# An attention-and-MLP kernel whose instruction order comes from a planner: VectorE units placed by bank, MLP output parked in SBUF, zero products in TensorE's pauses

## The chip, the cores and the metric

The kernel runs on one core of a Trainium2 chip. The metric is the device time of one execution in microseconds (us), lower is better. Three runs of the kernel before gave 899.79, 900.54 and 901.49 us; the median is 900.54 us.

## The reference, cut to what matters

```python
def _A_ref(x, wqkv, wo):                       # S = 2048 tokens, D = 512, H = 32 heads of Dh = 16
    q, k, v = split(x @ wqkv)
    p = softmax((q @ k.T) * Dh ** -0.5)        # per head, 2048 x 2048
    return merge_heads(p @ v) @ wo
def _B_ref(x, w1, b1, w2, b2):                 # F = 1792
    h = gelu(layernorm(x) @ w1 + b1)           # tanh form
    return h @ w2 + b2
xn = layernorm(x)
return x + _A_ref(xn, wqkv, wo) + _B_ref(xn, w1, b1, w2, b2)
```

So there are 32 x 2048 x 2048 exponentials, the two small products around each, and an MLP over the same tokens.

## The kernel before, in words

Work is cut into 32 groups: 4 quarters of 512 queries (`qt`), and in each 8 sets of 4 heads (`g`). For one group and one of 16 blocks of 128 keys (`k`) there are 4 score tiles of 128 x 512, one for each head. TensorE makes a score tile with one product of 32 rows (`qk`, from `kt` and `qz`); products of different heads stand in different rows of the array and run together. Most score tiles are exponentiated by ScalarE: two or three PSUM banks at a time, a *tile* of the plan (`build_tile`, banks 0 to 2 and 3 to 4 in turn, result in the 15 slots of `p_sb`). In groups 2 to 31 four of the sixteen key blocks (`KD`) go to VectorE instead: it makes the exponential from the bits of float16 numbers. One such block has 4 *units*: each reads one score tile out of PSUM and writes int16 (`f1`, result `x_sb`), and then four additions over all 4 heads (`f2`, results `tb_x` and `x_sb`) give five terms. The exponentials are multiplied with the values (`pv`, four products of 32 columns that run together, a *row* below) and gathered over a whole group in PSUM bank 6. After a group VectorE copies that bank out (`osb`), the sums of the softmax go through HBM and back to be inverted and spread over the partitions (`ldram`, `lc`, `rc`, `rdram`, `rlb`), and VectorE multiplies (`ont`).

Banks 5 and 7 (`misc`) serve everything else: the scores of the VectorE units, the projections, and the MLP. A resource `one` lets only one user other than the units hold a `misc` bank at a time. In each quarter the MLP makes 14 blocks of its hidden layer (`build_mlp`: four products each, VectorE adds the bias and writes `ht`), one gelu over all of it on ScalarE, and then `build_out` makes for each of 4 token blocks one chain of products into one bank: the input itself, 14 products of `ht` with `w2`, the bias, and 8 of the attention's heads with `wo`. VectorE copies the bank to `ot`, and it is stored. In the last quarter the chain leaves the last two heads to `build_final`, which adds them at the end.

Nothing of this order is fixed in the code. `_Plan` simulates the engines with estimated durations; at each step it takes, for each engine, the ready operation with the smallest `prio` among those that can start within `TOL` of the first, with a bonus `KEEP` for TensorE operations of the same kind as the last (scores, values, or dense). Which tile a unit rides on was fixed ahead (`rider`): its score product was issued with a tile's, and the tile then needed a free `misc` bank to start. Where `_Plan` finds TensorE idle, `fill` may put products with zeros there; before, only ahead of 15 us of the plan. On the chip each engine runs its instructions in the planned order, held by semaphores.

Of the kernel before, what the change touches and what calls it, by code (L numbers as in the profile page):

```python
# [22 lines left out]
P = 128  # L23
DH = 16
HS = 4
# [26 lines left out]
class _Op:  # L52

    __slots__ = ("eng", "dur", "fn", "ndeps", "outs", "prio", "acq", "rel", "lat", "ready", "end",
                 "done", "dense", "mode", "seq")
# [5 lines left out]
class _Plan:  # L61
# [9 lines left out]
    TOL = 0.2  # L71
    KEEP = 2.0
# [16 lines left out]
    def add(self, eng, dur, fn, deps=(), prio=0.0, acq=(), rel=(), lat=0.0, dense=0.0, nb=0.0,  # L89
            mode=None):  # L90
        op = _Op()
        op.eng, op.dur, op.fn, op.prio, op.lat, op.dense = eng, dur, fn, prio, lat, dense
# [12 lines left out]
        self.ops.append(op)  # L105
        return op
# [16 lines left out]
    def run(self):  # L123
# [5 lines left out]
        left = len(self.ops)  # L129
        self.mode = None  # L130
        while left:
# [20 lines left out]
            if op.eng == "PE" and self.fill is not None:  # L152
                for dur, fn in self.fill(free["PE"], t):
                    self.cur = "PE"
                    fn()
                    free["PE"] += dur
                t = max(t, free["PE"])
            ready[op.eng].remove(op)
            for res, key in op.acq:
# [5 lines left out]
            self.now = t  # L165
# [15 lines left out]
            if op.dense:  # L181
                self.dense_log.append((t, op.dense))
            lag = self.PELAT if op.eng == "PE" else self.LAT
            for o in op.outs:
# [4 lines left out]
            left -= 1  # L189
        self.free = free  # L190

    dense_log = ()
# [239 lines left out]
def kernel(  # L432
# [136 lines left out]
    OUT0, OUT1, HLO = 0.4, 0.7, 0.42  # L569
    LEAD = 7  # L570
    start = [T0]
    for g in range(NG):
        start.append(start[-1] + (31.0 if not KD_OF[g] else 24.0) + (1.1 if g % NS != 7 else 1.5))
# [365 lines left out]
    rider = {}  # L939
# [3 lines left out]
    todo = []  # L943
    for g in range(NG):
        t = tiles_of[g]
        nd = len(KD_OF[g])
        for y, k in enumerate(KD_OF[g]):
            todo.append((g, k, {0, 1, 2, 3}, t[0] + len(t) * y / nd - LEAD))
    for i, (b0, n, u0) in enumerate(tiles):
        if not todo or todo[0][3] > i:  # L950
            continue
        g, k, js, _ = todo[0]
        fits = js - {units[u][2] for u in range(u0, u0 + n)}
        if fits:
            j = min(fits, key=lambda j: (j - units[u0][2] - n) % HS)
            rider[i] = (g, k, j)
            js.discard(j)
            if not js:
                todo.pop(0)
    assert not todo  # L960

    def build_tile(i):
# [3 lines left out]
        gd, kd, jd = rider.get(i, (None, None, None))  # L966
        key = ("d", i)

        def fqk():
            for x, (g, k, j) in enumerate(us):  # L970
                qk(b0 + x, g, k, j)
            if kd is not None:
                qk(misc.bank(key), gd, kd, jd)
# [4 lines left out]
        acq = [(res[b0 + x], ("t", i)) for x in range(n)]  # L978
        if kd is not None:
            need_q(gd)  # L980
            deps.update(qk_deps(gd, kd))
            deps.add(va_op[NT - 1])
            acq.append((misc, key))
        q = add("PE", pen(1), fqk, list(deps) + [qk_prev[0]], dl - 43.0, acq=acq, mode="q")
# [3 lines left out]
        if kd is not None:  # L988
            qk_last.setdefault(gd, []).append(q)
            dve_unit(gd, kd, jd, q, dl, key)  # L990
# [17 lines left out]
    def build_pv(u0):  # L1008
        g, k, _ = units[u0]

        def fpv():
            pv(g, k, [(va[:, k, :], lambda j: p_sb[:, unit_slot[u0 + j], :])])
        o = add("PE", pen(1), fpv, set([unit_exp[u0 + j] for j in range(HS)]
                                       + [va_op[k], va_op[min(k + 1, NT - 1)]]),
                due(u0 + 4) - 37.0, acq=((o_ready, g),), mode="p")
        for j in range(HS):
            pv_of_unit[u0 + j] = o
        pv_ops[g].append(o)
# [4 lines left out]
    ib_of, p1_ops = {}, {}  # L1023

    def dve_unit(g, k, j, q, dl, key):
        if (g, k) not in ib_of:
            ib_of[g, k] = ib_n[0]
            ib_n[0] += 1
        n_ = ib_of[g, k]
        sl = n_ % NI  # L1030

        def f1():
            I(nc.vector.tensor_scalar(out=ib[sl][:, j, :], in0=ps[:, misc.bank(key), :],  # L1033
                                      scalar1=LEVEL, scalar2=0.0, op0=ALU.add, op1=ALU.max))
        ins = p1_ops.setdefault((g, k), [])
        ins.append(add("DVE", dve(QW), f1, [q] + list(ib_use.get(n_ - NI, ()))
                       + list(xn_op.values()), dl - 800.0, rel=(misc.giver(key),)))
        if len(ins) == HS:
            dve_terms(g, k, n_, ins, dl)

    def dve_terms(g, k, n_, ins, dl):
# [7 lines left out]
        for t in range(1, TERMS):  # L1049
# [8 lines left out]
            a = add("DVE", dve(HS * QW, 0.26), f2, ins + list(tb_use.get(x - NTB, ())), dl + t - 20.0)  # L1058
# [3 lines left out]
            if len(rows) == 2 or t == TERMS - 1:  # L1062
                o = add("PE", pen(len(rows)), lambda rows=rows: pv(g, k, rows),
                        deps + [va_op[NT - 1], vs_op[k]], dl + 5.0 - 37.0, acq=((o_ready, g),),
# [88 lines left out]
    def build_mlp(qt):  # L1153
        lo, hi = (qts(qt, 0.30), qts(qt, 0.78)) if qt == 0 else (qts(qt, HLO), qts(qt, 0.78))
# [46 lines left out]
        def fg():  # L1201
            for h0 in (0, half):
# [6 lines left out]
    def build_out(qt, gl):  # L1209
        del h_use[:]  # L1210
        last = qt == NQT - 1
        for c in range(TQ):
# [5 lines left out]
            if last:  # L1218
                pr = ts_(NG - 1, -0.8 + 0.35 * c)
                gs = gs[:-2]  # L1220
            xr = dma("SP", x_r[:, qi % 2, :], x2[qi * P:(qi + 1) * P, :],
                     list(x_use.get(qi - 2, ())), pr - 10, nb=pr - 20)
            steps = [(ident_bf[:], x_r[:, qi % 2, :])]
            steps += [(ht[:, fc, cs], w2_sb[:, fc, :]) for fc in range(FC)]
            steps += [(ones_bf[0:1, 0:P], b2_sb[0:1, :])]
            steps += [(ont[:, g % NON, cs], wo_pad[:, (g % NS) // 2, g % 2, :]) for g in gs]
            m = gl
            for f0 in range(0, len(steps), 3):
                part = steps[f0:f0 + 3]

                def fn(part=part, f0=f0, key=key, n=len(steps)):
                    for y, (a, b) in enumerate(part):
                        I(nc.tensor.matmul(ps[:, misc.bank(key), :], lhsT=a, rhs=b,  # L1233
                                           start=(f0 + y == 0), stop=(f0 + y == n - 1)))
                deps = [m]
                if f0 == 0:
                    deps += [xr, ld_w2, ld_b2] + [on_op[g] for g in gs] + ld_wo
                m = add("PE", mmd(len(part)), fn, deps, pr,
                        acq=((one, key), (misc, key)) if f0 == 0 else (), dense=float(len(part)))
                if f0 == 0:  # L1240
                    x_use[qi] = (m,)
                if f0 <= FC < f0 + 3 and c == TQ - 1:
                    h_use.append(m)
            for g in gs:
                ont_use.setdefault(g, []).append(m)
            if not last:
                e = add("DVE", dve(D), lambda qi=qi, key=key: I(nc.vector.tensor_copy(
                    ot[:, qi % 2, :], ps[:, misc.bank(key), :])), [m, ot_use.get(qi - 2)], pr - 500,
                    rel=(one, misc.giver(key)))
                ot_use[qi] = dma("SP", o2[qi * P:(qi + 1) * P, :], ot[:, qi % 2, :], (e,), pr)  # L1250
            else:
                acc_op[c] = add("DVE", dve(D), lambda c=c, key=key: I(nc.vector.tensor_copy(
                    acc[:, c, :], ps[:, misc.bank(key), :])), [m], pr - 500,
                    rel=(one, misc.giver(key)))
# [24 lines left out]
    gl = {0: build_mlp(0)}  # L1279
    ti = pend = 0  # L1280
    for g in range(NG):
        qt, s = divmod(g, NS)
        stop = end_unit[g]
# [9 lines left out]
        if s == (NS - 1 if qt < NQT - 1 else NS - 3):  # L1293
            build_out(qt, gl[qt])
            if qt + 1 < NQT:
                gl[qt + 1] = build_mlp(qt + 1)
# [3 lines left out]
    log = I.dense_log = []  # L1300

    def fill(t0, t1):
        got = []
        t = max(t0, 2.5)
        while t0 < T0 and t + 0.25 < t1:
            def fn():
                I(nc.tensor.matmul(ps[:, OB, :], lhsT=zeros_bf[:], rhs=ones_bf[:],
                                   start=True, stop=True))
            got.append((0.216, fn))
# [46 lines left out]
```

## Time and profile before

| | |
|---|---|
| median of 3 runs | 900.54 us |
| profiled execution, its own time | 901.28 us |
| its span, first to last instruction | 899.4 us |
| busy: TensorE, VectorE, ScalarE | 774.4, 773.4, 773.0 us (each 86% of the span) |
| granted TensorE clock, mean | 0.938 of full |

The rows below come from one profiled execution. A row of the timeline has the start, the length, the engine, the line of the kernel, what is written and read, and in brackets how long the engine had been idle and what ended that. PE is TensorE, DVE is VectorE, ACT is ScalarE, SP issues the DMAs. Rows that follow each other on an engine are merged and counted (x4). TensorE's busy time is modelled, and products overlap in it, so what a product costs is read from the distance of starts.

### The profile page before, as it was taken

What the parts mean: (1) busy time and instruction counts of PE and PEld (TensorE: products, weight loads), DVE (VectorE), ACT (ScalarE), POOL (GpSimd) and SP (SyncE); (2) the same over time, 40 slices, a digit from 0 to 9 for tenths busy, and PEclk for the clock granted to TensorE, in tenths of its full rate; (3) what the DMA queues carried; (4) which work ended last, traced back from release to release, by engine and by line L of the source; (5) the groups of instructions that cost most, each with busy time, mean ns of one, the idle gap of its engine ahead of it and who ended that gap; (6) DMA issues with size and microseconds to landing.
All of it is one profiled execution on the core that took longest, in us unless ns stands there. A gap on an engine that the chain in (4) does not pass through costs nothing.

```text
span 899.4 us, 17244 instructions
## 1 busy us (share of the span) xinstructions
PE 774.4 (86%) x6866; PEld 244.3 (27%) x6948; DVE 773.4 (86%) x1330; ACT 773.0 (86%) x667; POOL 53.1 (6%) x153
## 2 busy tenths in 40 slices
PE   8998889968889998986879987996878898899796
PEld 3332222212222232221222222321222222222222
DVE  8657999979998899996988899997888789999583
ACT  4896889999998889889998789889998789998792
POOL 2200000000000000000000000000000000000000
PEclk9997899989899999997899999998799999899898
DMA  5300121000000100110000010210000010021000
GB/s 164 100 1 19 28 57 26 15 13 20 20 20 26 43 26 18 42 28 19 19 20 26 20 36 15 48 38 19 3 20 30 26 38 19 9 60 32 19 20 28
DMA packets 54810, 27.65 MB, mean 31 GB/s; under 512 B 40645, under 2 KB 50630, under 8 KB 54722
## 3 DMA queue, kind: packets, MB, share of 16 engines
q1 hardware_dynamic: 52562, 24.76, 10.1%
q10 hardware_dynamic: 2160, 1.70, 0.6%
q8 instruction: 56, 0.92, 0.4%
q14 instruction: 32, 0.26, 0.1%
HBM read 23.85 MB, written 2.61 MB: 29 GB/s over the span
## 4 chain that ended last, share of the span: by engine, by line
DVE 36%; PE 32%; ACT 16%; issue 9%; DMA 6%; SPq 0%; POOL 0%; ACTq 0%; DVEq 0%
ACT p_sb L999 14%; DVE x_sb L1033 14%; PE ps L933 11%; PE ps L915 10%; DVE tb_x L1054 7%; PE ps L1233 7%; DMA rlb<-rdram 4%; DVE x_sb L1054 4%; DVE ht L1195 3%; ACT ht L1204 1%; PE ps L812 1%; DMA rdram<-rc 1%; DVE ont L1101 1%; DVE osb L1087 1%; PE ps L740 1%
## 5 line engine op out<-in xcount | busy, mean ns | idle before, releaser
L999 ACT ACTIVATE p_sb<-ps 128x1024 bf16<-128x1024 f32 (+1 forms) x640 | 732.6, 1234 | 99.4 <-PE ps L915 93.4
L1033 DVE TENSOR_SCALAR x_sb<-ps 128x512 int16<-128x512 f32 x480 | 323.9, 683 | 55.7 <-PE ps L915 54.9
L915 PE MATMUL ps<-qz,kt 32*128 32x512 bf16 x2048 | 282.2, 405 | 82.8 <-ACT p_sb L999 70.2
L1054 DVE TENSOR_SCALAR tb_x<-x_sb 128x2048 int16<-128x2048 int16 x320 | 215.6, 684 | 6.2 <-PE ps L933 4.4
L933 PE MATMUL ps<-p_sb,va 128*32 128x512 bf16 x1568 | 163.8, 410 | 0.2
L915 PEld LDWEIGHTS <-kt 32*128 32x128 bf16 x2048 | 75.6, 91 | 300.4 <-issue 295.6
L933 PE MATMUL ps<-tb_x,vs 128*32 128x512 f16 x1280 | 127.5, 410 | 7.1 <-DVE tb_x L1054 6.4
L1054 DVE TENSOR_SCALAR x_sb<-x_sb 128x2048 int16<-128x2048 int16 x160 | 109.3, 683 | 2.0 <-PE ps L933 1.3
L933 PEld LDWEIGHTS <-va 128*32 128x32 bf16 x2048 | 50.2, 95 | 128.1 <-issue 124.6
L933 PEld LDWEIGHTS <-vs 128*32 128x32 bf16 x1920 | 59.2, 98 | 83.6 <-issue 64.7
L933 PE MATMUL ps<-x_sb,vs 128*32 128x512 f16 x640 | 67.9, 412 | 3.1 <-DVE x_sb L1054 3.0
L1188 PE MATMUL ps<-yT,w_r 128*128 128x512 bf16 x194 | 56.4, 383 | 8.8 <-DVE x_sb L1033 5.7
L1108 POOL TENSOR_SCALAR okt<-lc 128x16 f32<-128x16 f32 x31 | 12.5, 404 | 785.9 <-DMA lc<-ldram 785.9
L1233 PE MATMUL ps<-w_sb,ht 128*128 128x512 bf16 x198 | 56.2, 391 | 2.7 <-issue 2.1
L933 PE MATMUL ps<-x_sb,va 128*32 128x512 f16 x480 | 51.4, 414 | 2.6 <-DVE osb L1087 2.5
L1195 DVE TENSOR_SCALAR ht<-ps,b_sb 128x512 bf16<-128x512 f32 x56 | 41.7, 744 | 1.0 <-PE ps L1188 0.8
L1101 DVE TENSOR_TENSOR ont<-osb,rlb 128x512 bf16<-128x512 f32 x31 | 21.3, 686 | 15.0 <-DMA rlb<-rdram 15.0
L1233 PE MATMUL ps<-wo_pad,ont 128*128 128x512 bf16 x113 | 31.3, 382 | 1.0 <-issue 1.0
L1188 PEld LDWEIGHTS <-w_r 128*128 128x128 bf16 x224 | 19.6, 97 | 38.9 <-issue 25.3
L1233 PEld LDWEIGHTS <-ht 128*128 128x128 bf16 x224 | 17.9, 98 | 32.0 <-issue 19.7
L1204 ACT ACTIVATE ht<-ht 128x3584 bf16<-128x3584 bf16 x8 | 25.1, 3183 | 0.0
L1087 DVE COPY osb<-ps 128x512 f32<-128x512 f32 x31 | 21.2, 684 | 4.5 <-PE ps L933 4.4
(88 smaller groups left out, 304.8 us busy)
## 6 DMA issues: line engine op xcount, KB each, us to landing
rlb<-rdram SPq DMA_DIRECT2D x31, 256.0 KB
w_r<-in_B_w_dram SPq DMA_DIRECT2D x56, 128.0 KB
x_r<-in_A_x_dram SPq DMA_DIRECT2D x16, 128.0 KB
w_sb<-in_B_w_dram SPq DMA_DIRECT2D x1, 1792.0 KB
out_dram<-ot SPq DMA_DIRECT2D x12, 128.0 KB
x_sb<-in_A_x_dram SPq DMA_DIRECT2D x2, 512.0 KB
wkv<-in_A_wqkv_dram ACTq DMA_DIRECT2D x1, 512.0 KB
x_sb<-in_A_x_dram ACTq DMA_DIRECT2D x1, 512.0 KB
```

Source lines behind the costliest of these rows:

```text
L915: I(nc.tensor.matmul(ps[:, bank, :], lhsT=kt[lo:lo + 32, s // 2, k * P:(k + 1) * P], rhs=qz[lo:lo + 32, (qt * NB + s // 2) % NQB, s % 2, : ...
L933: I(nc.tensor.matmul(ps[32 * j:32 * j + 32, o_bank[g], :], lhsT=vals[:, h * VS:h * VS + 32], rhs=wts(j), start=st, stop=(pv_left[g] == 0), ...
L999: I(nc.scalar.activation(p_sb[:, s0:s1, :].rearrange("p a b -> p (a b)"), ps[:, b0:b0 + n, :].rearrange("p a b -> p (a b)"), AF.Exp, scale ...
L1033: I(nc.vector.tensor_scalar(out=ib[sl][:, j, :], in0=ps[:, misc.bank(key), :], scalar1=LEVEL, scalar2=0.0, op0=ALU.add, op1=ALU.max))
L1054: I(nc.vector.tensor_scalar(out=tb[x % NTB].rearrange("p j q -> p (j q)"), in0=ib[sl].rearrange("p j q -> p (j q)"), scalar1=float(SHIFT[t ...
L1087: e0 = add("DVE", dve(QW), lambda: I(nc.vector.tensor_copy(osb[:, i2, :], ps[:, o_bank[g], :])), pvs + before, pr - 1000, rel=(o_ready if ...
L1101: e4 = add("DVE", dve(QW), lambda: I(nc.vector.tensor_tensor(out=ont[:, slot, :], in0=osb[:, i2, :], in1=rlb[:], op=ALU.mult)), [e3] + lis ...
L1108: I(nc.gpsimd.tensor_scalar(out=okt[:, 0, :], in0=lc[:, i2, :], scalar1=L_MIN, scalar2=None, op0=ALU.is_ge))
L1188: I(nc.tensor.matmul(ps[:, misc.bank(key), :], lhsT=w1_r[:, n % NW1, jc, :], rhs=yT[:, jc, :], start=(jc == 0), stop=(jc == JC - 1)))
L1195: I(nc.vector.tensor_scalar(out=ht[:, fc, :], in0=ps[:, misc.bank(key), :], scalar1=b1_sb[:, fc:fc + 1], scalar2=None, op0=ALU.add))
L1204: I(nc.scalar.activation(out=hv, in_=hv, func=AF.Gelu_apprx_tanh, scale=1.0))
L1233: I(nc.tensor.matmul(ps[:, misc.bank(key), :], lhsT=a, rhs=b, start=(f0 + y == 0), stop=(f0 + y == n - 1)))
```

## The change

- **Units.** `rider` is no longer fixed ahead. When a tile is scheduled, the function `ride` decides whether a unit goes with it: only when a `misc` bank is free at that time of the plan, unless the unit is late (`LATE`). While ScalarE is in gelu (`gelu_end`), units may go with no tile at all: operations marked `spare` that the plan may drop. `build_dve` builds a block's VectorE work ahead, without the number of the tile.
- **MLP output.** The chain of each token block is cut in two. `build_down` (input, 14 products with `w2`, bias) follows the gelu in the same quarter, and VectorE copies the bank to `acc` in SBUF (the space of `wkv`). `build_out` has the 8 head products alone, later; VectorE adds `acc` while it empties the bank. Chains are issued in parts of four products and no longer three. There are 16 more emptyings of a bank than before.
- **Zero products.** `fill` also works after the start: where the plan has TensorE idle, and either the pause is long or less than `NEED` products lie in the last 3.4 us, products with zeros are added into the open sum of bank 6.
- **Numbers of the plan.** `TOL`, `KEEP`, the times of the MLP (`HLO`, `HHI`, `DN0`, `DN1`, `OUT0`, `OUT1`) and the lead of each kind of operation change.

```diff
-    TOL = 0.2
-    KEEP = 2.0
+    TOL = 0.25
+    KEEP = 0.5
...
+    def ride(i, alone=None):
...
+        def f(_, take=False, give=None):
+            if alone is not None:
+                if take:
+                    g, k, js, _, late = todo[0]
+                    return attach(g, k, js, js, True, key, misc(key))
+                if (not todo or gelu_end[0] <= I.now or todo[0][3] - AHEAD > tile_now[0]
+                        or not all(o.done for o in qk_deps(*todo[0][:2]))):
+                    return None
+                free = misc(key)
+                return None if free is None or free >= gelu_end[0] else free
...
+            must = late - len(js) <= i
+            free = misc(key)
+            if not take:
+                return free if must else 0.0
+            if free is None or not (must or free <= I.now + 0.05):
+                return None
...
-        q = add("PE", pen(1), fqk, list(deps) + [qk_prev[0]], dl - 43.0, acq=acq, mode="q")
+        q = add("PE", pen(1), fqk, list(deps) + [qk_prev[0]], dl - QO, acq=acq, mode="q")
...
+    def build_down(qt, gl):
...
+            pr = qts(qt, DN0 + DN1 * c)
+            steps = [(ident_bf[:], x_r[:, qi % 2, :])]
+            steps += [(ht[:, fc, cs], w2_sb[:, fc, :]) for fc in range(FC)]
+            steps += [(ones_bf[0:1, 0:P], b2_sb[0:1, :])]
...
+            acc_op[c] = add("DVE", dve(D), lambda c=c, key=key: I(nc.vector.tensor_copy(
+                acc[:, c, :], ps[:, misc.bank(key), :])),
+                [m] + wait, pr - 500, rel=(one, misc.giver(key)))
...
+            steps = [(ont[:, g % NON, cs], wo_pad[:, (g % NS) // 2, g % 2, :]) for g in gs]
...
+            acc_op[c] = e = add("DVE", dve(D), lambda c=c, key=key, dst=dst: I(
+                nc.vector.tensor_tensor(out=dst, in0=ps[:, misc.bank(key), :], in1=acc[:, c, :],
+                                        op=ALU.add)),
...
-        while t0 < T0 and t + 0.25 < t1:
+        while t + 0.25 < t1:
+            if t0 > T0:
+                if o_open[0] is None:
+                    break
+                if (t1 - t0 < 2.0
+                        and sum(d for (a, d) in log[-40:] if a > t - 3.4) >= NEED):
+                    t += 0.1
+                    continue
...
```

Three places show how the order moves. Line numbers shift by some 50: `f1` is L1033 before and L1085 now, `f2` L1054 and L1108, `rc` L1094 and L1148, `ont` L1101 and L1155, the score products L915 and L921, the products of value rows L933 and L939.

VectorE around the gelu of the second quarter. Before:

```order
L1054 TENSOR_SCALAR x_sb<-x_sb 128x2048
L1054 TENSOR_SCALAR tb_x<-x_sb 128x2048 x2
L796 TENSOR_SCALAR qc<-ps 128x512
L801 TENSOR_SCALAR qz<-qc,mask 128x512 x2
L1101 TENSOR_TENSOR ont<-osb,rlb 128x512
L1033 TENSOR_SCALAR x_sb<-ps 128x512 x4
```

And now (`wkv` in the last row is the space that `acc` uses):

```order
L1108 TENSOR_SCALAR x_sb<-x_sb 128x2048
L1085 TENSOR_SCALAR x_sb<-ps 128x512 x2
L1108 TENSOR_SCALAR tb_x<-x_sb 128x2048
...
L1085 TENSOR_SCALAR x_sb<-ps 128x512 x2
L1108 TENSOR_SCALAR x_sb<-x_sb 128x2048
L1108 TENSOR_SCALAR tb_x<-x_sb 128x2048
L802 TENSOR_SCALAR qc<-ps 128x512
L1155 TENSOR_TENSOR ont<-osb,rlb 128x512
...
L1298 COPY wkv<-ps 128x512
```

Pairs of units stand in a row with the additions of their block between them, and the first emptying of an MLP chain follows shortly behind; before, no unit stood between the last additions and `ont`.

VectorE between the inverted sums `rc` and the multiplication `ont` of the 25th group before, with 7 instructions between:

```order
L1094 RECIPROCAL rc<-lc 128x16
L1033 TENSOR_SCALAR x_sb<-ps 128x512
L1054 TENSOR_SCALAR tb_x<-x_sb 128x2048 x2
L1033 TENSOR_SCALAR x_sb<-ps 128x512
L1054 TENSOR_SCALAR x_sb<-x_sb 128x2048
L1054 TENSOR_SCALAR tb_x<-x_sb 128x2048
L1033 TENSOR_SCALAR x_sb<-ps 128x512
L1101 TENSOR_TENSOR ont<-osb,rlb 128x512
```

And of the 23rd group now, with 26 instructions between:

```order
L1148 RECIPROCAL rc<-lc 128x16
L1108 TENSOR_SCALAR tb_x<-x_sb 128x2048
L1085 TENSOR_SCALAR x_sb<-ps 128x512 x2
...
L1108 TENSOR_SCALAR x_sb<-x_sb 128x2048
L1085 TENSOR_SCALAR x_sb<-ps 128x512
L1155 TENSOR_TENSOR ont<-osb,rlb 128x512
```

Over the 31 groups that go through HBM, 15 had at most 12 VectorE instructions between `rc` and `ont`; now 8 have.

VectorE at the very end, before:

```order
L1130 STREAM_TRANSPOSE ont<-on_t 128x512
L1135 TENSOR_SCALAR okl<-ta 128x16
...
L1141 TENSOR_REDUCE okr<-okl 128x1
L1252 COPY wkv<-ps 128x512
L1273 TENSOR_TENSOR yT<-ps,wkv 128x512 x4
```

And now:

```order
L1184 STREAM_TRANSPOSE ont<-on_t 128x512
L1189 TENSOR_SCALAR okl<-ta 128x16
...
L1195 TENSOR_REDUCE okr<-okl 128x1
L1344 TENSOR_TENSOR yT<-ps,wkv 128x512 x4
```

The emptying of the last MLP chain no longer stands between the last heads and the final sums.

More of the change, by code (lines that the diff above doesn't have):

```diff
@@ L128, in run @@
                 ready[op.eng].append(op)
-        left = len(self.ops)
+        left = sum(not op.spare for op in self.ops)
         self.mode = None
@@ L1220, in build_out @@
                 gs = gs[:-2]
[L1221 to L1243, printed above, removed]
@@ L1282 @@
         qt, s = divmod(g, NS)
+        for y in range(len(KD_OF[g])):
+            build_dve(g, y)
         stop = end_unit[g]
```

203 lines of the change are left out of this document (130 added, 73 removed).

## The prediction

> **What bounds the kernel now.** I began with the page's span and busy times, then asked the waits who waits for whom, then cut the span into stretches of about one group (19 or 20 tiles of ScalarE), and last read the timeline in the worst of them.
>
> ```profile
> span 899.4 us, 17244 instructions
> ...
> PE 774.4 (86%) x6866; PEld 244.3 (27%) x6948; DVE 773.4 (86%) x1330; ACT 773.0 (86%) x667; POOL 53.1 (6%) x153
> ```
>
> ```profile
> ACT p_sb L999 <- PE ps L915: 93.4, 145, 3.7
> PE ps L915 <- ACT p_sb L999: 70.2, 139, 5.2
> DVE x_sb L1033 <- PE ps L915: 54.9, 65, 5.4
> DVE ont L1101 <- DMA rlb<-rdram: 15.0, 11, 3.0
> PE ps L933 <- DVE osb L1087: 2.5, 8, 0.6
> ```
>
> The three engines are equally busy, so no total names the bound. The waits do: ScalarE idles 93.4 us for score products, TensorE 70.2 us for banks that ScalarE still reads, VectorE 54.9 us for unit scores. ScalarE's exponentials are the same 640 before and after; so the time falls only where ScalarE's idle time does, and I go by stretches (columns: length, then busy time and count of PE, weight loads, DVE, ACT and POOL, then the clock).
>
> ```profile
> 200.90:223.30 22.40, 19.45 (x195) 5.98 (x196) 19.85 (x35) 21.57 (x20) 1.55 (x4) 0.92 0.07 20
> ...
> 269.20:297.20 28.00, 27.24 (x243) 8.02 (x245) 23.93 (x40) 23.85 (x21) 1.67 (x4) 1.00 0.07 22
> 297.20:323.60 26.40, 24.92 (x230) 7.86 (x232) 23.66 (x44) 22.50 (x19) 1.31 (x4) 1.00 0.17 42
> 323.60:346.10 22.50, 19.19 (x206) 6.48 (x205) 21.18 (x36) 21.39 (x20) 1.74 (x4) 1.00 0.06 20
> 346.10:371.90 25.80, 23.54 (x217) 7.41 (x217) 25.52 (x42) 22.51 (x21) 1.66 (x4) 0.93 0.15 38
> 371.90:397.70 25.80, 23.84 (x219) 7.65 (x227) 25.80 (x45) 21.95 (x20) 0.90 (x4) 1.00 0.15 38
> ...
> 430.20:453.30 23.10, 18.84 (x191) 5.85 (x191) 21.12 (x36) 21.73 (x21) 1.40 (x4) 0.85 0.07 20
> 453.30:480.90 27.60, 24.07 (x216) 7.34 (x217) 23.04 (x40) 22.25 (x21) 1.40 (x4) 0.88 0.06 16
> 480.90:508.80 27.90, 26.04 (x229) 7.83 (x231) 22.80 (x38) 22.67 (x20) 1.78 (x4) 1.00 0.09 26
> 508.80:535.00 26.20, 25.05 (x228) 7.72 (x229) 23.41 (x43) 22.22 (x21) 0.94 (x4) 1.00 0.15 38
> ...
> 641.90:665.30 23.40, 19.43 (x191) 5.51 (x191) 18.71 (x33) 21.82 (x21) 1.34 (x4) 0.86 0.08 19
> 665.30:694.10 28.80, 25.20 (x220) 7.90 (x223) 24.81 (x43) 23.45 (x21) 0.91 (x4) 0.94 0.05 16
> 694.10:723.40 29.30, 26.11 (x235) 8.55 (x238) 22.11 (x36) 22.75 (x20) 1.77 (x4) 1.00 0.10 29
> ```
>
> Three kinds stand out. Without MLP work (from 200.9, 323.6, 430.2 and 641.9) ScalarE idles 0.83, 1.11, 1.37 and 1.58 us, 1.22 on average: ScalarE bounds them. While the hidden layer is made (346.1, 371.9) it idles 3.29 and 3.85 us, and VectorE is nearly full (25.80 of 25.80). In the seven stretches with the long output chains it idles 4.15, 3.90, 5.35, 5.23, 3.98, 5.35 and 6.55, together 34.5 us, with TensorE fullest; that is 26.0 over seven times 1.22. There lies the largest removable piece.
>
> **The change part by part.** *Chains.* By the order before, up to 45 products of output chains fell on 19 or 20 tiles (15, 45 and 36 in the second quarter's chains). Now 64 of a quarter's 96 follow gelu at once (12, 36 and 16), where units have been done ahead and about eight tiles carry none; the 32 head products come apart, 20 and 12. In the first quarter the copy into `acc` must wait for the last K projection, whose weights lie there; the order puts the four projections ahead of the chain, and only the chain's own bank would be held. What a product costs:
>
> ```profile
> 288.37 0.82 PE L1233 MATMUL ps<-w_sb,ht 128*128 128x512 bf16 x3
> ...
> 289.12 0.39 PE L915 MATMUL ps<-qz,kt 32*128 32x512 bf16 x3
> ...
> 289.44 0.46 PE L933 MATMUL ps<-p_sb,va 128*32 128x512 bf16 x4
> ```
>
> Three dense products and the change to scores take 0.75 us from start to start, a set of scores and the change to values 0.32: a product is 0.215, a change of kind 0.105. The products stay the same in number; what falls is their crowding. Some of these stretches also hold a stall of another kind:
>
> ```profile
> 709.63 0.69 DVE L1101 TENSOR_TENSOR ont<-osb,rlb 128x512 bf16<-128x512 f32 x1 [2.96 <-DMA rlb<-rdram]
> ...
> 710.98 0.37 PE L915 MATMUL ps<-qz,kt 32*128 32x512 bf16 x1 [2.21 <-DVE x_sb L1033]
> ...
> 712.86 2.37 ACT L999 ACTIVATE p_sb<-ps 128x1536 bf16<-128x1536 f32 x2 [2.97 <-PE ps L915]
> ```
>
> VectorE waits for the softmax sums from HBM; the unit behind it keeps its bank, TensorE stands before that unit's score, and ScalarE loses 2.97 us. The 15.0 us of such waits should halve, since 8 and no longer 15 groups have at most 12 VectorE instructions as cover. On SP, each of these DMAs still stands behind loads of `w_r` and stores; their number is the same, and the denominators' own four DMAs keep their order. I keep 10 of the 26.0 as what crowding remains (the new chain stretches priced at about a third of the old ones' 3.7 us each) and take **-16**; the ends are 0 and -26.
>
> *Gelu.* The first of the four:
>
> ```profile
> 178.68 1.28 ACT L1204 ACT_TABLE_LOAD   x1
> ...
> 179.97 6.27 ACT L1204 ACTIVATE ht<-ht 128x3584 bf16<-128x3584 bf16 x2
> ...
> 189.05 0.62 PE L915 MATMUL ps<-qz,kt 32*128 32x512 bf16 x4 [4.24 <-ACT p_sb L999]
> ...
> 189.75 0.69 DVE L1033 TENSOR_SCALAR x_sb<-ps 128x512 int16<-128x512 f32 x1 [4.18 <-PE ps L915]
> ```
>
> TensorE waits 4.24 and VectorE 4.18 us, four times a run. By the order, 31 units now stand beyond the first on their tile, nearly all in the gelus, so some 4 x 4.18 = 16.7 us of VectorE's time is won; ScalarE's own gelu time stays. Behind gelu ScalarE bounds, so alone this is worth nothing; it is the cover for the chains above. *Emptyings.* Sixteen more readings of a bank, priced by the nearest rows:
>
> ```profile
> L1252 DVE COPY wkv<-ps 128x512 f32<-128x512 f32 x4 | 2.7, 677 | 2.6 <-PE ps L1233 2.6
> L1273 DVE TENSOR_TENSOR yT<-ps,wkv 128x512 bf16<-128x512 f32 x4 | 2.5, 681 | 0.0
> ```
>
> 16 x 0.68 = 10.9 us of VectorE. The copies fall behind gelu, into time just won; the additions fall on the head products, part of them beside the hidden layer, where VectorE is full. I take **+3**, ends 0 and +10.9.
>
> *Start.* In this stretch ScalarE idles 16.00 - 7.34 = 8.66 us, 3.73 of it in one wait:
>
> ```profile
> 76.00:92.00 16.00, 12.03 (x66) 2.55 (x64) 11.61 (x19) 7.34 (x8) 0.91 (x4) 0.68 0.10 27
> ...
> 89.60 1.94 ACT L999 ACTIVATE p_sb<-ps 128x1024 bf16<-128x1024 f32 x2 [3.73 <-PE ps L915]
> ```
>
> Before, tile 61 was followed by a projection and 20 value products in one run, and five units rode before tile 64; now one does, and that run is gone. About half: **-4**, ends 0 and -8.7.
>
> *End.*
>
> ```profile
> 886.73 0.71 DVE L1130 STREAM_TRANSPOSE ont<-on_t 128x512 bf16<-128x512 bf16 x1
> ...
> 890.44 1.03 PE L1266 MATMUL ps<-wo_pad,ont 128*128 128x512 bf16 x4
> ...
> 891.25 2.48 DVE L1273 TENSOR_TENSOR yT<-ps,wkv 128x512 bf16<-128x512 f32 x4
> ```
>
> The last heads are ready at 887.44, but TensorE is in the last chain until 890.44. That chain is now earlier; the final products can start at once, so the additions start 3 us sooner: **-3**, ends 0 and -3.7.
>
> *Zero products.* There are 59 more (90 against 31), 14 of them on the gelus' tiles, under the 4.24 us wait. The other 45 cost 0.215 and a change, 0.32, at most 14.4 us if TensorE is never idle where the plan says so. Their use would be the clock:
>
> ```profile
> 429.42 0.40 PE L915 MATMUL ps<-qz,kt 32*128 32x512 bf16 x4 [0.62 <-ACT p_sb L999]
> ...
> 430.34 0.61 PE L915 MATMUL ps<-qz,kt 32*128 32x512 bf16 x3 [0.52 <-ACT p_sb L999]
> ```
>
> The clock halves here with no pause over 0.62 us near. But the stretches at 0.85 and 1.00 (430.2 and 323.6) differ by 0.26 us of ScalarE idle only, so a full clock everywhere is worth some 2 us. Net **+1**, ends -2 and +14.4. [...] *Order.* `TOL`, `KEEP` and the offsets let scores pass other kinds sooner. Changes of kind in the order, zeros left out, go from 1233 to 1195, 38 x 0.105 = 4 us of TensorE, mostly off the path: 0, ends -4 and +4.
>
> Sum: -16 + 3 - 4 - 3 + 1 = -19, against the profiled execution's 901.28: 882.3. That execution is 0.7 above the median of 900.54, so I say 882.
>
> **The rivals.** *Crowding only moves* (chance 0.20). The chains' products are as many, and the hidden layer's stretches (3.3 to 3.9 idle) keep theirs; if dense work costs ScalarE the same wherever it stands, the -16 shrinks to the halved denominator waits, about -5: 893. For it: idle grows with TensorE's busy time over all the rows. Against: the stretches with 27 and 26 busy are worse than in proportion.
>
> *The gather bank* (0.17), the slower side. Units that are late or go ahead make a group's value products uneven: between 112 and 156 products per 19 or 20 tiles now, 120 to 132 before, from the third such stretch on. Bank 6 is handed on only after a group's last row; if that is late, the next group's value products wait, the 15 slots fill in some six tiles, and ScalarE stops. Now a handover costs TensorE 2.5 us in 8 cases. If each of 30 handovers cost ScalarE 1 us it would be +30: 912. It decides from 19 / 30 = 0.6 us each.
>
> *Zeros in the way* (0.08). All 45 on the path, +14.4 for +1: 895. For it: TensorE is fullest where zeros are not, but the plan's pauses need not be the chip's.
>
> *Everything fits* (0.12). Chains at their end (-26) and the start too (-8.7): 882 - 10 - 5 = 867.
>
> **How the numbers follow.** The forecast case keeps 0.43, own range 873 to 891 (chains from -24 to -8). Faster by over 0.2%, which is about what a measurement can tell from no change, means below 898.7: the forecast, the fitting case, nearly all of the moved crowding and of the zeros, 0.76. Within 0.2%: 0.06, from their upper ends and the lower end of the gather bank. Slower: 0.18, the gather bank and some of the zeros. The range of 8 in 10 leaves out half of the fitting case and most of the gather bank: 867 to 904.
>
> **What would show it.** Right: the stretches behind gelu take about 23 to 24 us for 19 tiles while chains run; the waits of ScalarE for scores fall from 93.4 to about 75, those of `ont` for `rlb` to 6 to 9; VectorE has no wait of 4 us behind gelu; the final additions start within 1 us of the last transpose. Wrong: value products that wait for `osb`, VectorE at its full length in stretches with head products, or ScalarE's waits unchanged in sum.

## The result and the profile after

The changed kernel took 876.41 us (median of 4 runs, 875.44 to 878.26) against 900.16 us before (4 runs, 898.79 to 901.49): a ratio of 0.9739, 95% interval 0.9715 to 0.9762. Forecast were 882 us and 867 to 904. Two single executions, one of the kernel before (2053.4 us) and one of the split with zero products (1581.16 us), were far slower than all others; times and ratios below leave them out.

The page of the changed kernel, span and busy times, and from its waits (engine and line, what it waited for, total us, times, longest):

```profile
span 875.3 us, 17469 instructions
...
PE 789.1 (90%) x7007; PEld 248.6 (28%) x7007; DVE 780.0 (89%) x1346; ACT 771.8 (88%) x667; POOL 55.7 (6%) x153
```

```profile
ACT p_sb L1046 <- PE ps L921: 69.8, 133, 1.5
...
DVE x_sb L1085 <- PE ps L921: 31.8, 35, 2.5
PE ps L921 <- ACT p_sb L1046: 30.6, 89, 1.1
...
DVE ont L1155 <- DMA rlb<-rdram: 7.0, 5, 2.7
...
PE ps L939 <- DVE osb L1141: 4.9, 9, 1.0
```

ScalarE's busy time is the same; its waits for scores fell from 93.4 to 69.8 us, by 23.6, and the longest is 1.5 instead of 3.7 us. Some 3 us of this came back elsewhere (ahead of `xnT` at the start it waits 8.2 us, not 4.7). The span lost 24.1 us: the last tile ends at 862.9 us and no longer at 883.3, and what lies behind it takes 12.4 us and no longer 16.2. Waits for the spread sums fell from 15.0 to 7.0, those for the gather bank rose only from 2.5 to 4.9.

Stretches of 19 or 20 tiles of the changed kernel (length; busy time and count of PE, weight loads, DVE, ACT, POOL; clock):

```profile
174.70:201.10 26.40, 23.38 (x207) 7.06 (x206) 20.58 (x35) 22.38 (x21) 1.93 (x4) 0.94 0.06 17
201.10:225.70 24.60, 23.84 (x234) 7.30 (x231) 21.93 (x38) 22.25 (x21) 1.33 (x4) 1.00 0.06 19
...
296.80:323.30 26.50, 25.02 (x232) 8.01 (x232) 26.43 (x45) 22.44 (x20) 1.24 (x4) 1.00 0.16 42
323.30:349.70 26.40, 25.25 (x217) 7.70 (x216) 26.26 (x46) 22.16 (x20) 1.92 (x4) 1.00 0.20 47
382.20:405.20 23.00, 22.55 (x210) 7.19 (x213) 16.79 (x28) 21.85 (x21) 1.28 (x4) 1.00 0.07 19
405.20:430.10 24.90, 22.57 (x216) 6.87 (x212) 21.63 (x37) 23.11 (x21) 0.97 (x4) 1.00 0.04 13
...
587.90:611.70 23.80, 23.35 (x226) 7.56 (x224) 18.63 (x32) 22.04 (x20) 1.54 (x4) 1.00 0.07 19
611.70:635.20 23.50, 21.59 (x201) 6.31 (x199) 21.08 (x36) 22.21 (x19) 1.02 (x4) 0.93 0.06 19
...
702.30:729.60 27.30, 25.76 (x233) 8.03 (x229) 26.30 (x45) 22.20 (x20) 1.34 (x4) 1.00 0.16 45
787.60:812.60 25.00, 23.85 (x227) 8.07 (x227) 19.49 (x34) 23.00 (x21) 1.58 (x4) 1.00 0.06 18
```

In the last three quarters the stretches behind gelu that hold the chains with `w2` (from 382.2, 405.2, 587.9, 611.7, 787.6) leave ScalarE idle 1.15, 1.79, 1.76, 1.29 and 2.00 us, where chain stretches before left 3.90 to 6.55. In the first quarter (174.7, 201.1), where the last K projections stand beside the chain, it idles 4.02 and 2.35. Where the hidden layer is made, beside head products (296.8, 702.3) or without them (323.3), it idles 4.06, 5.10 and 4.24, and VectorE is full (26.43 of 26.50). Before, the hidden layer's stretches (346.1, 371.9) left 3.29 and 3.85. So a part of the idle time that left the chains' stretches stands beside the head products now.

The start in its window, and the end in the timeline:

```profile
72.00:87.50 15.50, 14.22 (x92) 4.36 (x91) 9.81 (x17) 13.37 (x15) 0.91 (x4) 1.00 0.02 3
```

```profile
865.49 0.71 DVE L1184 STREAM_TRANSPOSE ont<-on_t 128x512 bf16<-128x512 bf16 x1
...
866.25 1.04 PE L1337 MATMUL ps<-wo_pad,ont 128*128 128x512 bf16 x4 [1.49 <-DVE ont L1184]
...
866.75 2.48 DVE L1344 TENSOR_TENSOR yT<-ps,wkv 128x512 bf16<-128x512 f32 x4
```

In this window ScalarE idles 2.13 us ahead of tile 64, in the one before 8.66. The final additions begin 0.55 us after the last transpose ends, not 3.81.

### The profile page after: what moved, and what is told of

It is laid out like the page before. It is cut to its first block, busy times and chain, and to the rows that moved or that the text cites. A ratio compares the mean times of both kernels' runs of the same rounds, so it can differ in the third digit from the quotient of the medians.

```text
span 875.3 us, 17469 instructions
## 1 busy us (share of the span) xinstructions
PE 789.1 (90%) x7007; PEld 248.6 (28%) x7007; DVE 780.0 (89%) x1346; ACT 771.8 (88%) x667; POOL 55.7 (6%) x153
## 4 chain that ended last, share of the span: by engine, by line
DVE 53%; PE 25%; ACT 10%; issue 8%; DMA 3%; POOL 0%; SPq 0%; DVEq 0%; ACTq 0%
DVE x_sb L1085 20%; DVE tb_x L1108 13%; ACT p_sb L1046 10%; PE ps L939 8%; PE ps L921 7%; DVE x_sb L1108 6%; PE ps L1272 5%; DVE ht L1249 4%; DMA rlb<-rdram 2%; DVE ont L1155 1%; DVE osb L1141 1%; PE ps L746 1%; PE ps L818 1%; PE ps L1390 1%; DVE stats L651 1%
## 5 line engine op out<-in xcount | busy, mean ns | idle before, releaser
L1046 ACT ACTIVATE p_sb<-ps 128x1024 bf16<-128x1024 f32 (+1 forms) x640 | 731.2, 1232 | 76.8 <-PE ps L921 69.8
L1085 DVE TENSOR_SCALAR x_sb<-ps 128x512 int16<-128x512 f32 x480 | 324.2, 689 | 32.7 <-PE ps L921 31.8
L921 PE MATMUL ps<-qz,kt 32*128 32x512 bf16 x2048 | 285.5, 389 | 43.2 <-ACT p_sb L1046 30.6
L1108 DVE TENSOR_SCALAR tb_x<-x_sb 128x2048 int16<-128x2048 int16 x320 | 217.7, 690 | 4.9 <-PE ps L939 3.4
L939 PE MATMUL ps<-p_sb,va 128*32 128x512 bf16 x1568 | 153.4, 394 | 4.5 <-DVE osb L1141 4.4
L921 PEld LDWEIGHTS <-kt 32*128 32x128 bf16 x2048 | 76.1, 91 | 247.9 <-issue 240.7
L939 PE MATMUL ps<-tb_x,vs 128*32 128x512 f16 x1280 | 121.2, 391 | 9.5 <-DVE tb_x L1108 8.4
L1108 DVE TENSOR_SCALAR x_sb<-x_sb 128x2048 int16<-128x2048 int16 x160 | 110.4, 690 | 1.9 <-PE ps L939 1.1
L939 PEld LDWEIGHTS <-va 128*32 128x32 bf16 x2048 | 50.7, 95 | 117.2 <-issue 108.1
L939 PEld LDWEIGHTS <-vs 128*32 128x32 bf16 x1920 | 56.0, 95 | 96.1 <-issue 82.4
L939 PE MATMUL ps<-x_sb,vs 128*32 128x512 f16 x640 | 64.5, 391 | 5.6 <-DVE x_sb L1108 5.0
L1162 POOL TENSOR_SCALAR okt<-lc 128x16 f32<-128x16 f32 x31 | 17.0, 548 | 761.0 <-DMA lc<-ldram 761.0
L1272 PE MATMUL ps<-w_sb,ht 128*128 128x512 bf16 x224 | 59.5, 383 | 0.0
L939 PE MATMUL ps<-x_sb,va 128*32 128x512 f16 x480 | 48.9, 397 | 0.5 <-DVE osb L1141 0.5
L1390 PE MATMUL ps<-ones_bf,zeros_bf 128*128 128x512 bf16 x90 | 33.9, 455 | 1.5 <-DVE ones_bf L613 1.5
L1242 PEld LDWEIGHTS <-w_r 128*128 128x128 bf16 x224 | 19.2, 97 | 37.6 <-issue 23.6
L1155 DVE TENSOR_TENSOR ont<-osb,rlb 128x512 bf16<-128x512 f32 x31 | 21.4, 690 | 7.0 <-DMA rlb<-rdram 7.0
```

The source lines that it names most:

```text
L921: I(nc.tensor.matmul(ps[:, bank, :], lhsT=kt[lo:lo + 32, s // 2, k * P:(k + 1) * P], rhs=qz[lo:lo + 32, (qt * NB + s // 2) % NQB, s % 2, : ...
L939: I(nc.tensor.matmul(ps[32 * j:32 * j + 32, o_bank[g], :], lhsT=vals[:, h * VS:h * VS + 32], rhs=wts(j), start=st, stop=(pv_left[g] == 0), ...
L1046: I(nc.scalar.activation(p_sb[:, s0:s1, :].rearrange("p a b -> p (a b)"), ps[:, b0:b0 + n, :].rearrange("p a b -> p (a b)"), AF.Exp, scale ...
L1108: I(nc.vector.tensor_scalar(out=tb[x % NTB].rearrange("p j q -> p (j q)"), in0=ib[sl].rearrange("p j q -> p (j q)"), scalar1=float(SHIFT[t ...
L1155: e4 = add("DVE", dve(QW), lambda: I(nc.vector.tensor_tensor(out=ont[:, slot, :], in0=osb[:, i2, :], in1=rlb[:], op=ALU.mult)), [e3] + lis ...
L1162: I(nc.gpsimd.tensor_scalar(out=okt[:, 0, :], in0=lc[:, i2, :], scalar1=L_MIN, scalar2=None, op0=ALU.is_ge))
```

## The experiments

All ratios are to the kernel before, in runs on the same chip, with 95% intervals. 0.004 of ratio is 3.6 us. The expectations speak of these theories. A: the gain comes from spreading the chains (the split and the freer riding), as forecast. B: it comes from the clock, which the zero products hold up. C: the zero products stand in the way. D: the gain comes from the units that ride free or go alone. E: it comes from the numbers of the plan.

**Zero products left out of the stream, order unchanged.**

```diff
             def fn(opened=o_open[0]):
+                if opened is not None:
+                    return
```

> The changed kernel with the same planned order, but the 59 zero products after the start are left out of TensorE's stream; the result does not depend on them. Theory A (the gain comes from spreading the chains; zeros cost about as much as they bring): 873 to 878 us, within 3 us of the changed kernel's 876.4. Theory B (the gain comes from the clock, which rose from 0.938 to 0.97): 884 us or more, with a clock back near 0.94 and ScalarE's waits for scores up by 8 us or more. Theory C (zeros stand in the way): 870 us or less.

878.74 us, ratio 0.9779 (0.9746 to 0.9812); the clock is 0.952 to 0.968 in the six runs.

```profile
ACT p_sb L1046 <- PE ps L921: 72.3, 128, 1.9
```

Nearest to Theory A, 0.7 us past the end of its range: 0.0040 more than the changed kernel, some 3.6 us, with intervals that overlap. The clock did not go back to 0.94, so something else of the change had raised it as well.

**The split chain alone, on the kernel before.** `build_down`, the short `build_out` and the new MLP times put into the kernel before:

```diff
-    OUT0, OUT1, HLO = 0.4, 0.7, 0.42
+    OUT0, OUT1 = 1.15, 0.3
+    HLO, HHI, DN0, DN1 = 0.15, 0.56, 0.56, 0.11
...
+            build_down(qt, build_mlp(qt))
```

> The kernel before with one part of the change: the MLP chain cut in two, with the new times of the MLP and the bank emptied to SBUF; units ride as fixed ahead, no zero products, old numbers of the plan. Theory A (spreading the chains is the main piece, but needs units done ahead during gelu as cover): 885 to 892 us, a third to two thirds of the gain. Theory B (clock) and theory D (the free units are the gain): 898 us or more, since the 16 added emptyings cost up to 10.9 us of VectorE and nothing else changes.

898.40 us, ratio 0.9977 (0.9954 to 1.0000). Theory A missed, and the number is the one of Theories B and D: the largest term of the forecast brings some 2 us when it stands alone. About twenty tiles around the second quarter's gelu, first of this kernel, then of the kernel before:

```profile
356.40:392.50 36.10, 30.15 (x232) 8.66 (x235) 25.39 (x44) 31.51 (x25) 0.91 (x4) 0.86 0.04 12
```

```profile
397.70:430.10 32.40, 22.30 (x206) 6.46 (x200) 25.25 (x43) 31.78 (x24) 0.91 (x4) 0.84 0.05 14
```

Before, no product with `w2` stands there, and ScalarE idles 0.62 us (32.40 - 31.78). Here 32 of them follow gelu, and it idles 4.59 (36.10 - 31.51), as much as chain stretches idled before. About 3 us of that lie behind gelu. By this stretch the chain takes idle time along when it is moved by itself. What the split brings lies at the end: in the profiled executions the last tile ends at 885.4 us here and at 883.3 before, and from there to the end of the span it takes 12.2 us here and 16.2 before.

**The chain joined again, in the changed kernel.** The code of `build_out` and the MLP times of before, the rest as changed:

```diff
-            build_down(qt, build_mlp(qt))
+            build_out(qt, gl[qt])
...
-    OUT0, OUT1 = 1.15, 0.3
-    HLO, HHI, DN0, DN1 = 0.15, 0.56, 0.56, 0.11
+    OUT0, OUT1, HLO, HHI = 0.4, 0.7, 0.42, 0.78
```

> The changed kernel with the MLP as before: one chain of input, 14 products, bias and 8 head products, emptied once, at the old times; units ride freely and alone, zero products stay. Theory A: most of the gain is lost, 890 to 897 us, and stretches with chains again show ScalarE idle for 4 us or more. Theory B and D: 880 us or less, since clock and free units stay and 16 emptyings are saved.

889.37 us, ratio 0.9889 (0.9868 to 0.9910): 13.5 us over the changed kernel, a little under Theory A's range. Its stretches with joined chains:

```profile
264.70:293.10 28.40, 27.27 (x241) 8.49 (x240) 23.05 (x39) 23.85 (x20) 0.90 (x4) 1.00 0.07 21
293.10:319.80 26.70, 25.13 (x228) 8.09 (x229) 23.03 (x42) 22.69 (x20) 0.94 (x4) 1.00 0.13 37
```

They are those of before again (ScalarE idle 4.55 and 4.01). But the time is not lost there. ScalarE's last tiles, and what TensorE does behind them:

```profile
855.53 6.88 ACT L1045 ACTIVATE p_sb<-ps 128x1536 bf16<-128x1536 f32 x6 [0.20 <-PE ps L920]
...
867.19 3.18 PE L1303 MATMUL ps<-w_sb,ht 128*128 128x512 bf16 x14
...
872.58 3.19 PE L1303 MATMUL ps<-w_sb,ht 128*128 128x512 bf16 x14
```

The last tile ends at 862.4 us, and in the changed kernel at 862.9. ScalarE's waits for scores are 71.0 us here and 69.8 there. Two chains run behind the last tile, so from its end to the end of the span it takes 22.3 us and not 12.4: that is 9.9 us of the loss. Between these two executions the split is worth nothing among the tiles; of the 13.5 us at most 3 to 4 are left for it there. (The planner puts 77 zero products after the start here, 59 in the changed kernel.)

**Riding as before.** A tile with a unit due waits for a bank, and no unit goes alone:

```diff
-    for x in range(10 * NQT):
+    for x in range(0):
...
-            must = late - len(js) <= i
+            must = True
```

> The changed kernel in which a tile with a unit due waits for a bank, and no unit goes alone during gelu, as before the change; split chains and zeros stay. Theory A: the cover behind gelu is missing, 880 to 886 us, VectorE idle 4 us in each gelu again. Theory D (the free units are the gain): 890 us or more. If units don't matter at all: 876 us.

882.18 us, ratio 0.9811 (0.9795 to 0.9827), 6.5 us over. This is Theory A's number, but the loss is not where Theory A had it: ahead of tile 64 alone, this kernel idles ScalarE for 9.43 us again (19.50 - 10.07), and tile 64 comes at 95.5 instead of 87.5.

```profile
76.00:95.50 19.50, 16.40 (x88) 3.81 (x88) 12.30 (x20) 10.07 (x12) 0.92 (x4) 0.74 0.05 16
```

From tile 64 on this kernel loses nothing against the changed one. It has 119 zero products after the start, not 59, which may have stood in for part of it.

**No units alone, riding free.** Only the first line of the edit above.

> The changed kernel without units that go alone during gelu; riding stays free. The fixed riding lost 8 us ahead of tile 64 and nothing after it. If alone units are worth nothing by themselves: 875 to 878 us. If they are the cover for the chains, as predicted: 880 us or more, with stretches behind gelu over 24 us.

879.75 us, ratio 0.9743 (0.9717 to 0.9769): not to be told from the changed kernel's 0.9739. Tile 64 comes at 87.35 us, so it is the free riding that mends the start. VectorE waits behind gelu again, and it costs nothing that can be measured:

```profile
371.30 0.69 DVE L1085 TENSOR_SCALAR x_sb<-ps 128x512 int16<-128x512 f32 x1 [4.05 <-PE ps L921]
```

The planner puts more zero products in this kernel (130 and not 59 after the start), so they may have stood in for part of it.

**The plan's numbers alone, on the kernel before.**

```diff
-    TOL = 0.2
-    KEEP = 2.0
+    TOL = 0.25
+    KEEP = 0.5
...
-        ... dl - 43.0 ... dl + t - 20.0 ... dl + 5.0 - 37.0
+        ... dl - 45.5 ... dl + t - 25.0 ... dl + 5.0 - 39.5
```

The nominal length of a group changes with them, from 24.0 to 24.75 us.

> The kernel before with the new numbers of the plan alone (TOL 0.25, KEEP 0.5, a group's nominal length 25.85 us, scores and additions 2.5 and 5 us earlier in rank); the MLP, the riding and the zero products are as before. Theory E, formed after the split alone gave 898.4 and the fixed riding lost only at the start: the numbers carry the middle of the run, 882 to 888 us. Theory A' (the numbers are worth something only with the split, which needs scores to pass the chains' parts): 894 to 899 us.

898.31 us, ratio 0.9961 (0.9939 to 0.9982). Theory E falls: 3.5 us.

**The old numbers in the changed kernel** (the same edit backwards).

> The changed kernel with the old numbers of the plan (TOL 0.2, KEEP 2.0, nominal length, offsets). Theory E: 890 us or more, the loss in the middle of the run, with ScalarE's waits for scores back above 85 us. Prediction's step (order numbers cost 0, ends -4 and +4): 872 to 881 us.

870.84 us, ratio 0.9666 (0.9639 to 0.9692). Both expectations missed (the second by 1.2 us), since it is faster than the changed kernel by 0.0073, 6.6 us. With the rest of the change in place the new numbers cost.

**Zero products alone, on the kernel before.** The new `fill`, with its log of TensorE's work:

```diff
-        while t0 < T0 and t + 0.25 < t1:
+        while t + 0.25 < t1:
+            if t0 > T0:
...
```

> The kernel before with zero products in the plan's pauses (145 after the start) and nothing else. Over repeated runs of one kernel the time falls by 3 to 6 us for each 0.01 that the mean granted clock rises. Theory B (the clock is a cause): clock from 0.935 to 0.97 or more, 885 to 892 us. Theory A (the clock follows the flow of work, and zeros are paid for in TensorE's time): clock up, but 898 to 904 us.

884.35 us, ratio 0.9836 (0.9809 to 0.9863), clock 0.989 in the profiled run: 15 us from zero products alone. This is Theory B's case, 0.65 us better than its range, and the plainest picture of all runs, because everything else in the order stays. Waits and stretches, the same tiles as the rows of before at 323.6, 371.9, 430.2, 641.9 and 694.1:

```profile
ACT p_sb L999 <- PE ps L915: 76.2, 128, 2.5
...
DVE ont L1101 <- DMA rlb<-rdram: 12.4, 11, 1.9
```

```profile
320.00:342.50 22.50, 19.19 (x206) 6.82 (x207) 21.20 (x36) 21.42 (x20) 1.59 (x4) 1.00 0.07 20
368.40:394.30 25.90, 23.93 (x222) 7.69 (x227) 25.90 (x45) 22.00 (x21) 1.42 (x4) 1.00 0.16 38
425.90:447.50 21.60, 17.06 (x193) 6.21 (x194) 20.67 (x36) 21.60 (x21) 1.36 (x4) 1.00 0.08 20
...
631.30:652.70 21.40, 17.01 (x192) 5.99 (x193) 18.89 (x33) 21.40 (x21) 1.32 (x4) 1.00 0.07 21
680.30:707.90 27.60, 26.12 (x235) 8.55 (x238) 22.11 (x38) 22.79 (x20) 1.97 (x4) 1.00 0.11 31
```

Where the clock stood at 1.00 before, the length stays (22.50 and 22.50; 25.80 and 25.90). Where it stood at 0.85 and 0.86, 23.10 becomes 21.60 and 23.40 becomes 21.40, and ScalarE never idles. The stretch at 694.1 had the full clock too, and fell from 29.30 to 27.60. There it is the wait for the spread sums that shrank, at the same two instructions as the rows of before at 709.63 and 712.86:

```profile
694.12 0.69 DVE L1101 TENSOR_TENSOR ont<-osb,rlb 128x512 bf16<-128x512 f32 x1 [1.21 <-DMA rlb<-rdram]
...
697.35 2.37 ACT L999 ACTIVATE p_sb<-ps 128x1536 bf16<-128x1536 f32 x2 [1.22 <-PE ps L915]
```

VectorE's wait fell from 2.96 to 1.21 us and ScalarE's from 2.97 to 1.22. About 90 of the 145 products stand within 12 us of the start of a gelu, and the rest in pauses elsewhere; no run separates the two.

**Split and zero products, riding and numbers of before.** Both edits above.

> The kernel before with the split chain and zero products (138 after the start), old numbers and fixed riding. The split alone gave 898.4. Theory B: 880 to 888 us, as the split leaves TensorE more pauses in which the clock fell, and the zeros take that away. Theory A: 894 us or more; then what made the split pay is the free riding.

882.11 us, ratio 0.9807 (0.9780 to 0.9834). This is Theory B's number, but the split again adds next to nothing to zeros alone (0.9836, overlapping). One wait has grown:

```profile
DVE ont L1102 <- DMA rlb<-rdram: 23.1, 12, 5.1
```

It was 12.4 us with zeros alone. With the split and fixed riding it is 19.9 (split alone), 23.1 and 19.7 us (riding as before), and 14 or 15 groups have at most 12 VectorE instructions between `rc` and `ont`. With free riding and joined chains it is 12.9 us. With the split and free riding it is 4.5 to 7.0 us, and in the changed kernel 8 groups have so few. So it takes both together.

**Old numbers, split and free riding, zero products left out.**

> The changed kernel with the old numbers of the plan (870.8 us with its zero products), its 65 zero products after the start left out, same planned order. Theory A: 871 to 876 us, so split and free riding together carry some 27 us. Theory B: 882 us or more.

874.79 us, ratio 0.9732 (0.9702 to 0.9762), clock 0.966: as Theory A had it. The zeros are worth 0.0066, 6 us, beside split and free riding, against 15 us in the kernel before.

**The sums' latency as measured, in the changed kernel.**

```diff
-                 [e3, last_rlb[0]], pr - 500, lat=2.2)
+                 [e3, last_rlb[0]], pr - 500, lat=5.0)
```

Seven transfers into `rlb` on the chain that ended last took 4.73 to 5.45 us in the kernel before, and four 4.78 to 5.30 us in the changed one.

> The changed kernel with one planned latency set to what the trace shows for the spread of the inverted sums (4.7 to 5.4 us from issue to landing; the plan has 2.2). VectorE's multiplication is then planned later. If the 7.0 us of waits of ont on rlb reach ScalarE one for one: 870 us; half: 873; if the later place only moves the wait or shifts the plan at random: 874 to 879.

868.50 us, ratio 0.9627 (0.9601 to 0.9652): 10 us less than the changed kernel, more than the 7.0 us of waits. No instruction of `ont` waits for `rlb` any more, and ScalarE's waits fall on:

```profile
ACT p_sb L1046 <- PE ps L921: 62.3, 115, 1.6
```

A new number also shifts the rest of the plan, so not all of the 10 us is the wait.

**Both: old numbers and the measured latency.**

> The changed kernel with the old numbers of the plan and with the latency of the spread sums as the trace shows it: the two edits that each beat the changed kernel (870.8 and 868.5 us). If their gains add, 862 to 864 us; if both work on the same idle time of ScalarE, 867 to 871.

866.60 us, ratio 0.9627 (0.9604 to 0.9650). The gains do not add: beside the old numbers the latency brings 0.0039, 3.5 us, with intervals that overlap. This kernel and the one with the latency alone are the fastest, 3.7% under the kernel before and 1.1% under the changed one.

By parts (S split, R free riding, Z zero products, N new numbers; S R without Z and S R N have the zeros' time in the plan but not in the stream):

| parts | ratio | last tile ends, us | behind it, us |
|---|---|---|---|
| none, the kernel before | 1 | 883.3 | 16.2 |
| S | 0.9977 | 885.4 | 12.2 |
| N | 0.9961 | 874.2 | 16.3 |
| Z | 0.9836 | 863.0 | 16.9 |
| S Z | 0.9807 | 868.0 | 12.3 |
| S R | 0.9732 | 857.6 | 11.7 |
| S R N | 0.9779 | 864.5 | 12.1 |
| S Z N | 0.9811 | 869.8 | 12.0 |
| R Z N | 0.9889 | 862.4 | 22.3 |
| S R Z | 0.9666 | 852.4 | 12.0 |
| S R Z N, the change | 0.9739 | 862.9 | 12.4 |

The last two columns are from the one profiled execution of each kernel, which for N, S R and S R Z was the fastest of its runs; so the third column scatters by some us, and the fourth hardly. Three pairs differ by the split: none and S, Z and S Z, R Z N and the change. In each the split shortens what lies behind the last tile, by 4.0, 4.6 and 9.9 us, and in none does the last tile end sooner. Three pairs differ by the riding: with the old numbers it is worth 0.0245 without zeros (S and S R, 22 us) and 0.0141 with them (S Z and S R Z, 12.7 us), and with the new numbers 0.0072 (6.5 us). No run has the free riding without the split on the old numbers. Among the tiles, then, the gain is that of the zeros (Theory B) and of the riding (Theory D), which overlap; the split, the first half of Theory A, brings the end.

## Why the prediction was right, and where its steps were not

The direction and the range were right: 876.4 lies 5.6 us under the point, and ScalarE's waits for scores fell to 69.8 us where about 75 was said. The account behind the point was not. The mechanism of its largest term failed, and two parts that it priced low, zero products and free riding, are large. That the errors nearly cancel is luck.

- **Chains, -16.** The step that failed. Moving the chains was to take 16 us of idle time from ScalarE. The stretches with `w2` do idle less (1.15 to 2.00 us in the last three quarters), but where head products stand beside the hidden layer it is 4.06 and 5.10. Over the whole run ScalarE idles 76.8 us ahead of its tiles, and 77.4 with the chains joined and all else as changed; the last tile ends at 862.9 and 862.4. So this term came out as the rival "crowding only moves" has it. The 13.5 us that joining costs are of the forecast's size by accident: 9.9 of them lie behind the last tile.
- **Zero products, +1.** It failed too. The prediction compared ScalarE's idle time at clock 0.85 (1.37 us, from 430.2) with a stretch at 1.00 (1.11 us, from 323.6), took both to be without MLP work, and read 0.26 us from it. But the second holds 11 products of an output chain (their row stands below the list). It stays at 22.50 us when zeros are added, while the first loses 1.5 us and its idle time vanishes. Alone the zeros bring 15 us, where +1 was said; beside split and free riding 6 us with the old numbers and 3.6, not clear of noise, with the new, where the clock was higher without zeros already (0.952 to 0.970, and 0.923 to 0.939 in the kernel before).
- **Free riding.** The prediction gave it a price of its own at the start only, and otherwise took units done ahead as cover for the chains. Beside the split it is worth 22 us, or 12.7 with zeros, on the old numbers, more than the start holds. How much of that comes through the waits for the spread sums, through the clock or through the units' banks, no run separates.
- **Units alone in gelu as cover.** Not borne out: without them the time is the same, though that kernel has 130 zero products in place of 59. VectorE's waits in the four gelus were 4.18, 2.32, 2.30 and 5.38 us before, 14.2 in sum, where four times the first gave 16.7.
- **Denominators.** 15.0 us of waits became 7.0, as forecast (6 to 9). It takes the split and the free riding together: with one of them alone these waits are 12.9 to 23.1 us. Removing those 7.0 by the measured latency brought 10 us beside the new numbers, and 3.5 us, not clear of noise, beside the old, where they were 6.3. So what such a wait costs stays open.
- **Emptyings, +3.** No run separates this term. VectorE at its full length beside head products was named as a sign of being wrong, and it came (26.43 of 26.50).
- **Start, -4.** Tile 64 starts at 87.5 instead of 92.0: -4.5. Free riding is the cause: with fixed riding it is 95.5, with free riding and no unit alone 87.35.
- **End, -3.** 3.81 us became 0.55 between the last transpose and the sums: -3.3. This is the split's doing.
- **Numbers of the plan, 0 with ends -4 and +4.** -3.5 alone, within the ends, and +6.6 in the change, outside them. The changes of kind, counted from the weight loads of the two traces, are 1234 and 1228; a fall by 38 isn't found there.

The products of the output chain (L1233) in the stretch that the prediction took to be without MLP work; length, their time and number, the same of their weight loads, clock:

```profile
323.60:346.10 22.50, 3.22 (x11) 0.84 (x12) 1.00 0.06 20
```

In the kernel before the clock stands at half behind a long pause of TensorE, and elsewhere without one. Two such stretches:

```profile
348.30:351.70 3.40, 3.04 (x27) 0.82 (x26) 3.40 (x5) 2.57 (x3) 0.00 (x0) 0.50 0.05 9
416.50:426.80 10.30, 8.87 (x65) 1.99 (x62) 7.15 (x11) 9.85 (x9) 0.00 (x0) 0.50 0.00 0
```

The second begins 1.3 us after the end of TensorE's pause of 3.94 us at a gelu. In the 10 us ahead of the first, at the full clock, TensorE had not paused for more than 0.62 us, and had been busy for 6.51. So the clock falls here without a long pause too; what makes it fall, no run shows.

Of the other rivals, the gather bank did not come (4.9 us of waits by TensorE), and zeros were not in the way: leaving them out made neither kernel faster.

## What to carry to other kernels

Judge a low clock by comparing the same tiles with and without it, not two stretches that merely look alike. Where an order is planned ahead with estimated durations, put the measured latency of each transfer into the plan: here one such number brought 10 us beside one set of the plan's numbers, and 3.5 beside another. Parts of a change that relieve the same idle time don't add, so test each with the others in place. And when a part is taken out again, look in the trace for the place where the time went: here most of it lay behind the last tile, and not where the part was meant to help.

## What the runs showed of the hardware

- The granted clock varies between runs of one and the same program, and in most kernels here the time goes with it. Four of the six runs of the changed kernel without zero products in the stream: 875.4 us at a mean clock of 0.966, 876.3 at 0.968, 878.4 at 0.963, 885.1 at 0.952; over all six the time is 5.8 us shorter for each 0.01 of clock. Over 16 runs of the kernel before beside them the correlation is -0.72, and the time is 3.2 us shorter for each 0.01 of clock. Not every kernel shows it: of the six runs with the joined chain the one with the lowest clock, 0.931, was the fastest (885.75 us). Such figures alone don't say which follows which; the zero products alone, with an order otherwise unchanged, raised the clock from 0.927 to 0.939 up to 0.979 to 0.989 in every run, and took 15 us off.
- 145 products with zeros, added to the kernel before, raised its clock and made it faster by these 15 us, though they take TensorE's time too. In the changed kernel's trace three of them in a row (from 777.98) take 0.82 us where one takes 0.39, so 0.215 us from one to the next; 145 times that is some 31 us, an estimate.
